# SyncE issue times that depend on pair sums in a build-time planner, and new order rules for its last quarter

## Chip, cores and metric

The kernel runs on one core of a Trainium2 chip. The metric is the time of one execution in device microseconds (us); the number compared is the median of several runs. One further execution is taken with the hardware profiler, and its trace is what the profile below is made of.

## The reference, cut to what is computed

```python
xn = layernorm(x)                       # x: 1 x 2048 x 640
q = (xn @ wq)  -> 32 heads of 20;  k = xn @ wk;  v = xn @ wv     # one K and V for all heads
p = softmax(q k^T * 20**-0.5)           # 32 x 2048 x 2048
attn = (p v, heads side by side) @ wo
h = relu(xn @ w1 + b1) ** 2             # 640 -> 1536
return x + attn + (h @ w2 + b2)
```

All inputs and the output are bf16.

## The kernel before, in words

**Tiles.** The attention is cut into 32 *blocks*, one for each of 4 query chunks (512 queries) times 8 groups of 4 heads. A block has 16 key tiles x 4 heads = 64 score tiles of 128 x 512, so 2048 in all. TensorE makes a score tile in one of the 8 PSUM banks; two paths turn it into exponentials:

- **ScalarE path**: steps `QK0` to `QK695` make 2 tiles each, and one ACTIVATE (L1020) takes the exponential of both. 1392 tiles go this way. `PV<block>_<key tile>` are the matmuls that multiply them with V.
- **Set path**: 164 *sets* of 4 tiles (one key tile, 4 heads). `DQK<set>_<head>` makes the scores, `D1_<set>_<i>` on VectorE (L1232) writes a scaled integer whose bits are a rough bf16 exponential, and three *passes* `P1` to `P3` add constants to those bits, on GpSimd (`int64_add`, L1252) or on VectorE (L1254). The four terms are multiplied with V or with a scaled V and added up in PSUM (`DPV<block>_<key tile>_<term>`). A **pair sum** `AD0` or `AD3` adds two of the terms before that, which saves one `DPV`: as a DMA that accumulates 512 KB from SBUF into SBUF, issued by GpSimd (L1267), or on VectorE (L1272).

**End of a block.** `TN` (VectorE, L1101) copies the block's result out of PSUM. Then a chain through memory divides by the sums of the softmax: SyncE issues `SM` (L1103, sums to DRAM) and 4 or 5 `OM` (L1124, the heads' rows to their places); `SL` (L1105) reads the sums back, spread over 128 partitions; `RC` (VectorE reciprocal, L1107) inverts them; `RS` (L1108) writes them out; `BC` (L1130) broadcasts them; `CM` (VectorE, L1137) multiplies. SyncE is one in-order queue of DMA issues, which also has `QD` (L733, queries to their places), `FR` (L766), `OD` (L814, output rows) and `XD30` (L1094). Blocks 30 and 31 are divided on VectorE without memory (L1082 to L1099).

**Other work.** Between attention matmuls TensorE fills in the projections (`QC`), the first MLP matmul (`FFN`, evacuated by `RL`, squared by `SQ`), and `OUT16` to `OUT23`, each of 17 chunks of 4 matmuls (MLP second matmul and `wo`), evacuated by `OE` (L838). The last four row tiles end in the tail: `OF<row>_<half>_<chunk>` (5 chunks of 4 matmuls for each of 8 halves), `PA` (L1327) and `OFe` (L1332, L1334).

**What sets the order.** Nothing is ordered by hand around the change. When the kernel is built, a planner (the `while True` loop, and `commit`, L194) plays the engines forward with a planned duration for each operation, picks the next operation by planned start and priority, and appends it to its engine's list. The chip then runs each list strictly in order, with semaphore waits where data comes from another engine or a DMA. Planned durations do not reach the chip; they only decide the order. On SyncE they are constants: 0.62 for `SM`, 0.6 for `SL`, `RS` and `BC`, 0.95 for `OM`, 0.9 for `QD`, 0.45 for `OD`, 0.7 for `FR`. `dma_free` is the planned time until which the DMA engines are taken by pair sums (2.73 us each, `ADGAP`) and other transfers.

`RULES` holds, for each 10 us *stage* of the planned ScalarE time, the planner's parameters that differ from `DEFAULTS`: priorities (`PVA`, `PVD`, `SQP`), how many sets may be open (`NOPEN`), how many pair sums per set go by DMA (`ADDM`) or to VectorE (`ADDN`), how readily passes go to VectorE (`PBIAS`), and others.

Of the kernel before, what the change touches and what calls it, by code (L numbers as in the profile page):

```python
# [28 lines left out]
EPS = 1e-5  # L29
# [9 lines left out]
def _pl(z):  # L39
# [61 lines left out]
KEEP = 3  # L101
# [50 lines left out]
         53: {'DRATE': 0.8, 'ND': 1, 'ADPM': 2.4},
         54: {'DRATE': 0.8, 'EPS': 0.03, 'R3': 9, 'PVA': 1, 'ND': 1, 'ADPM': 2.4},
         55: {'DRATE': 0.8, 'PP': 0.9, 'QKP': -0.5},
         56: {'DRATE': 0.8, 'M1T': 0, 'ADDN': 0, 'ADDB': 1, 'SQP': 0.7, 'ADDM': 0},
         57: {'DRATE': 0.8, 'M1T': 0, 'ADDN': 0, 'ADDB': 1, 'SQP': 0.7, 'ADDM': 0},
         58: {'PVA': 0.9},
         59: {'DRATE': 0.95, 'IDLE': 0.15, 'URG': 4, 'EPS': 0.03, 'ADP': 2, 'D1P': 0.3, 'PP': 4, 'SQP': 0.7, 'ND': 1, 'KEEP': 0, 'ADPM': 2.4, 'KEEPX': 2, 'DVL': 2.4},
         60: {'DLAST': 2, 'EPS': 0.06, 'DQP': 1.5, 'ADDM': 1},
         61: {'EVP': 0.8, 'DGAP': 0, 'DRATE': 0.95, 'IDLE': 0.15, 'URG': 4, 'ADP': 5, 'PVA': 0.9, 'PP': 4, 'KEEP': 0, 'ADPM': 2.4, 'DVL': 2.4},  # L160
         62: {'EVP': 0.3, 'DGAP': 1.5, 'DRATE': 0.95, 'BEHIND': 0.12, 'IDLE': 0.15, 'NOPEN': 3, 'EPS': 0.06, 'MRG': 1, 'M1': 0, 'ADP': 3.5, 'JIT': 0.7, 'PVA': 0.9, 'D1P': 0.3, 'PP': 4, 'SQP': 2, 'DQP': 0.5, 'KEEP': 2, 'ADDM': 1.5, 'ADPM': 2.4, 'KEEPX': -1, 'DVL': 0.9, 'P2': 2},
         63: {'EVP': 0.3, 'DGAP': 1.5, 'DRATE': 0.95, 'BEHIND': 0.12, 'IDLE': 0.15, 'NOPEN': 3, 'EPS': 0.06, 'MRG': 0, 'M1': 0, 'ADP': 5, 'JIT': 0.7, 'PVA': 0.9, 'D1P': 0.3, 'PP': 4, 'SQP': 2, 'DQP': 0.5, 'KEEP': 1, 'ADDM': 1.5, 'ADPM': 2.4, 'KEEPX': -1, 'DVL': 0.9, 'P2': 2},
# [11 lines left out]
MPRIO = 0.9  # L174
BEHIND = 0.3
IDLE = 0.3
# [21 lines left out]
                M1T=2, ADDN=0, ADDB=0, ADP=0.9, JIT=0.9, R3=9, PVA=1, PVD=1.05, D1P=1, PP=2.5, SQP=0.7, DQP=3, QKP=0, ND=3, WARM=0.72,  # L198
                KEEP=1, ADDM=0.8, ADPM=0.9, KEEPM=0, KEEPX=4, DVL=1.2, P2=0)
# [66 lines left out]
def bass_parallel_sum__grouped_kv_mqa__dense_activation_squared_relu__prompt_kernel(nc, A_x, A_wq, A_wk, A_wv, A_wo, B_x, B_w1, B_b1, B_w2, B_b2, out):  # L266
    es = ExitStack()
    with es:
# [1099 lines left out]
        while True:  # L1368
# [313 lines left out]
```

## Time and profile before

| what | value |
|---|---|
| median of 3 runs (lowest to highest) | 669.46 us (669.13 to 669.87) |
| the profiled execution's own time | 670.66 us |
| its span, first to last instruction | 668.8 us |
| mean granted TensorE clock | 0.997 |
| pair sums by DMA | 67 + 56 + 5 of 512 KB, and 2 more from x_sb to tmore |

The profile's span is 1.9 us shorter than the execution it belongs to, and that execution is 1.2 us longer than the median. Busy shares are averages over the span; what ends a stretch is read from the idle time in front of an instruction, and the name behind the arrow there is what released it. "SPq" rows are SyncE's DMA issues: their duration is the issue, not the transfer.

### The profile page before, as it was taken

How to read it: one execution, taken by the hardware profiler on the slowest of the kernel's cores; microseconds unless marked ns; L12 is line 12 of the kernel's file. 1: busy time of each engine (PE TensorE's matmuls, PEld its weight loads, DVE VectorE, ACT ScalarE, POOL GpSimd, SP SyncE). 2: the span in 40 equal slices, each digit the busy share in tenths (PEclk: the TensorE clock that was granted, in tenths of full speed). 3: DMA queues.
4: the chain of work that ended last, by engine and by line, in shares of the span. 5: the costliest groups of instructions: out<-in, count | busy, mean ns of one | idle time of the engine just before them, and what ended most of it. 6: DMA issues, size and time to landing. Idle time of an engine off the chain costs nothing.

```text
span 668.8 us, 22416 instructions
## 1 busy us (share of the span) xinstructions
PE 661.0 (99%) x9602; PEld 210.7 (32%) x9603; DVE 602.8 (90%) x1081; ACT 651.4 (97%) x719; POOL 578.5 (87%) x592
## 2 busy tenths in 40 slices
PE   8999999999999999999999999999999999999898
PEld 4532222333322223333332222333332222223245
DVE  8979999999999999999989999988999999998654
ACT  6999999999999999999999999999999999999895
POOL 1619999999999999999899999999998998999761
PEclk9999999999999999999999999999999999999999
DMA  8897755787877987777788676668786976177875
GB/s 253 257 248 173 161 125 98 161 176 159 178 157 140 192 164 154 158 150 164 143 173 166 121 139 137 134 143 162 146 168 134 180 146 122 24 147 161 173 155 124
DMA packets 54360, 104.71 MB, mean 157 GB/s; under 512 B 16108, under 2 KB 31356, under 8 KB 54196
## 3 DMA queue, kind: packets, MB, share of 16 engines
q0 software_dynamic: 19376, 70.79, 56.8%
q1 hardware_dynamic: 34308, 32.11, 16.9%
q8 instruction: 75, 1.23, 0.8%
q10 hardware_dynamic: 576, 0.38, 0.2%
q14 instruction: 25, 0.20, 0.1%
HBM read 23.26 MB, written 10.01 MB: 50 GB/s over the span
## 4 chain that ended last, share of the span: by engine, by line
PE 88%; POOL 4%; DVE 3%; DMA 3%; SPq 1%; issue 1%; DVEq 0%; POOLq 0%
PE ps L429 86%; POOL x_sb L1252 2%; POOL tmore L1252 2%; DMA x_sb<-tmore 1%; PE ps L604 1%; DMA tmore<-tmore 1%; DVE tmore L1232 1%; PE ps L633 1%; SPq L1130 1%; DMA R<-drs 1%; SPq L1124 1%; DVE hT_tmp L753 0%; POOL tmore L1267 0%; POOL x_sb L1267 0%; PE ps L663 0%
## 5 line engine op out<-in xcount | busy, mean ns | idle before, releaser
L1020 ACT ACTIVATE PT<-ps 128x1024 bf16<-128x1024 f32 x696 | 642.2, 1066 | 5.1 <-PE ps L429 4.7
L1232 DVE TENSOR_SCALAR tmore<-ps 128x512 uint16<-128x512 f32 x656 | 424.5, 683 | 36.1 <-PE ps L429 28.1
L1252 POOL INT64_ADD tmore<-tmore x220 | 241.7, 1199 | 31.4 <-DVE QCr L707 10.2
L429 PE MATMUL ps<-qT,kT 20*128 20x512 bf16 x2048 | 265.2, 385 | 0.1
L1252 POOL INT64_ADD x_sb<-tmore x217 | 240.5, 1224 | 17.2 <-PE ps L429 7.2
L429 PEld LDWEIGHTS ps<-qT,kT 20*128 20x128 bf16 x2048 | 66.3, 91 | 254.1 <-ACT PT L1020 220.6
L429 PE MATMUL ps<-PT,vx 128*32 128x512 bf16 x1392 | 133.0, 388 | 0.0
L429 PE MATMUL ps<-w_sb,big 128*32 128x320 bf16 x1536 | 77.4, 305 | 2.0 <-DVE tmore L1232 2.0
L429 PE MATMUL ps<-xnT,w_sb 128*32 128x512 bf16 x960 | 77.3, 383 | 0.3 <-DVE tmore L1232 0.2
L1267 POOL DMA_DIRECT2D tmore<-tmore x67 | 68.4, 1036 | 3.3 <-POOL tmore L1252 2.1
L1267 POOL DMA_DIRECT2D x_sb<-tmore x56 | 62.0, 1123 | 2.1 <-POOL x_sb L1252 2.1
L429 PE MATMUL ps<-tmore,vxs 128*32 128x512 bf16 x632 | 57.3, 382 | 0.0
L429 PE MATMUL ps<-x_sb,vxs 128*32 128x512 bf16 x624 | 56.0, 382 | 0.3 <-POOL x_sb L1252 0.3
L429 PEld LDWEIGHTS ps<-PT,vx 128*32 128x32 bf16 x1392 | 33.4, 93 | 63.8 <-issue 58.0
L429 PE MATMUL ps<-tmore,vx 128*32 128x512 bf16 x512 | 48.7, 382 | 0.0
L429 PEld LDWEIGHTS ps<-w_sb,big 128*32 128x32 bf16 x1536 | 33.9, 96 | 30.7 <-issue 18.4
L753 DVE TENSOR_SCALAR hT_tmp<-ps,b1col 128x512 bf16<-128x512 f32 x48 | 35.6, 741 | 1.1 <-PE ps L429 1.0
L429 PE MATMUL ps<-xnT,wq_sb 128*32 128x512 bf16 (+2 forms) x480 | 33.3, 356 | 0.0
L429 PE MATMUL ps<-x_sb,vx 128*32 128x512 bf16 x328 | 32.1, 382 | 0.0
L429 PE MATMUL ps<-wo_c,OC 128*32 128x320 bf16 x576 | 29.8, 301 | 0.0
L429 PEld LDWEIGHTS ps<-xnT,w_sb 128*32 128x32 bf16 x960 | 18.3, 94 | 26.8 <-issue 20.6
L1254 DVE TENSOR_SCALAR x_sb<-tmore 128x2048 uint16<-128x2048 uint16 x28 | 22.0, 790 | 0.0
(97 smaller groups left out, 318.9 us busy)
## 6 DMA issues: line engine op xcount, KB each, us to landing
tmore<-tmore POOLq DMA_DIRECT2D x67, 512.0 KB, 5.5
x_sb<-tmore POOLq DMA_DIRECT2D x56, 512.0 KB, 5.6
w_sb<-in_B_w_dram SPq DMA_DIRECT2D x8, 480.0 KB, 11.5
big<-OR SPq DMA_DIRECT2D x71, 40.0 KB
xb<-in_A_x_dram SPq DMA_DIRECT2D x1, 2560.0 KB, 12.6
xb<-b2r POOLq DMA_DIRECT2D x1, 2560.0 KB, 19.9
xr<-xb SPq DMA_DIRECT2D x16, 160.0 KB, 4.3
x_sb<-x_sb POOLq DMA_DIRECT2D x5, 512.0 KB, 4.8
```

Source lines behind the costliest of these rows:

```text
L429: return lambda e: e.matmul(out_, l, r, start=start, stop=stop, tile_position=tp, skip_group_check=loose)
L604: return [lambda e: e.matmul(ps[:, PVB, :], ones_bf[:, :], hT_tmp[:, 0, :], start=True, stop=True)]
L633: return [(lambda e, dt=dt: e.transpose(out=psbf(bk)[:, dt * 128:(dt + 1) * 128], in_=xn_sb[:, st, dt:D:DT], identity=ident[:])) for dt in ...
L753: o = Op(f"RL{qc}_{f}", "DVE", 0.66, [lambda e: e.tensor_scalar(out=hT_tmp[:, k % 2, :], in0=ps[:, bk, :], scalar1=b1col[:, f:f + 1], scal ...
L1020: return Op(f"ACT{st_['j']}", "ACT", ACB + ACM * n, [lambda e: e.activation(out=PT[:, s0:s0 + n, :], in_=ps[:, b0:b0 + (n - 1) * db + 1:db ...
L1124: dd = wide(op(f"OM{b}_{j}", "SP", 0.95, lambda e, p0=p0, n=n, sl=sl, j=j, o0=o0: e.dma_start(cbuf(2 * sl)[p0:p0 + n, :], OR[32 * j + o0:3 ...
L1130: bc = wide(op(f"BC{b}_{j0}", "SP", 0.6, lambda e, p0=p0, n=n, m=m, sl=sl, j0=j0: e.dma_start(cbuf(2 * sl + 1)[p0:p0 + n, :], drs[b, 1][51 ...
L1232: d1 = op(f"D1_{n}_{i}", "DVE", 0.60, lambda e: e.tensor_scalar(out=L[:, cs].bitcast(U16), in0=ps[:, bank, :], scalar1=XA, scalar2=XB, op0 ...
L1252: fn = lambda e, T=T, j=j: e.int64_add(out=T.bitcast(I64), in0=L.bitcast(I64), in1=TSTEP * j * 0x0001000100010001)
L1254: fn = lambda e, T=T, j=j: e.tensor_scalar(out=T.bitcast(U16), in0=L.bitcast(U16), scalar1=TSTEP * j, scalar2=None, op0=ALU.add)
L1267: p = op(f"AD{a}_{n}", "POOL", ADDUR, lambda e, src=src, dst=dst: e.dma_start(dst, src, accum_op=ALU.add), dp + [ad_last.get(k)], dma=adse ...
```

## The change

Two things change in the planner; no operation's code changes.

1. **SyncE durations.** In `commit`, each SyncE operation with a planned start after 560 us gets its planned duration multiplied: by 1.3 if `dma_free` lies 1.0 to 2.9 us, or at least 4.0 us, ahead of the start, and by 0.84 otherwise.
2. **Rules.** The entries of `RULES` for stages 50 to 66 (planned ScalarE time from 490 us on) are replaced; stage 52 now has none.

```diff
+SPF, SPG, SPT = 1.3, 0.84, 560.0
 DWQ, DWO, DWB, DWS, DWM, DWOD, DOFF = 0.02, 0.22, 0.16, 0.02, 0.16, 1.0, 1.28
...
-         50: {'DGAP': 0.3, 'M1T': 0, 'PVD': 1.2, 'DVL': 0.9},
...
-         65: {'MPRIO': 0.9, 'BEHIND': 0.3, 'IDLE': 0.6, 'MRG': 0, 'KEEPX': 1},
-         66: {'MPRIO': 0.9, 'BEHIND': 0.3, 'IDLE': 0.6, 'MRG': 0, 'KEEPX': 1}}
+         50: {'EVP': 0.3, 'DGAP': 1.5, 'DRATE': 0.95, 'BEHIND': 0.12, 'IDLE': 0.15, 'NOPEN': 3, ...
+         51: {'EVP': 0.8, 'PBIAS': 3, 'DRATE': 0.95, 'NOPEN': 3, 'M1T': 1.2, 'ADP': 3.5, 'JIT': 0.8, ...
...
+         62: {'ADDN': 0.5},
...
+         65: {'EVP': 0.8, 'DGAP': 0.8, 'DLAST': 6, 'DRATE': 0.95, 'BEHIND': 0.12, 'IDLE': 0.3, 'URG': 2, ...
+         66: {'ADDB': 1, 'P2': 1}}
...
             if op.eng == "PE":
                 pe_mode[0] = op.mode
                 pe_log.append((s, s + op.dur))
+            if op.eng == "SP" and s > SPT:
+                op.dur *= SPF if 1.0 <= dma_free[0] - s < 2.9 or dma_free[0] - s >= 4.0 else SPG
             op.start, op.fin = s, s + op.dur
```

In the two built programs the lists are the same up to `QK523` on TensorE, the end of block 23 on VectorE, set 125 on GpSimd and `OM23_2` on SyncE. Behind that every list is in another order. ScalarE's list is the same throughout. The number of steps (696), of sets (164), of operations on SyncE (501) is the same.

More of the change, by code (lines that the diff above doesn't have):

```diff
@@ L148 @@
          49: {'EVP': 0.3, 'DGAP': 0.8, 'DLAST': 6, 'DRATE': 0.95, 'BEHIND': 0.12, 'IDLE': 0.3, 'URG': 2, 'EPS': 0.06, 'MRG': 1, 'M1T': 1.2, 'JIT': 0.8, 'PVA': 0.9, 'ND': 2, 'KEEP': 0, 'KEEPM': 2, 'KEEPX': -1, 'DVL': 99},
-         50: {'DGAP': 0.3, 'M1T': 0, 'PVD': 1.2, 'DVL': 0.9},
-         51: {'EVP': 0.8, 'DRATE': 0.95, 'URG': 4, 'M1T': 1.2, 'ADP': 3.5, 'JIT': 0.7, 'PVA': 0.9, 'D1P': 0.5, 'SQP': 3, 'ND': 2, 'KEEPM': 2, 'KEEPX': 1},
-         52: {'EVP': 0.8, 'DRATE': 0.95, 'NOPEN': 3, 'M1T': 1.2, 'ADP': 3.5, 'JIT': 0.8, 'PVA': 0.9, 'SQP': 3, 'ND': 2, 'KEEPX': 4},
@@ L152 @@
[L152 to L162, printed above, removed]
@@ L163 @@
-         64: {'EVP': 0.3, 'DGAP': 0.8, 'DLAST': 6, 'DRATE': 0.95, 'BEHIND': 0.12, 'IDLE': 0.3, 'EPS': 0.06, 'MRG': 1, 'M1T': 1.2, 'ADDN': 0.2, 'JIT': 0.8, 'PVA': 0.9, 'D1P': 0.5, 'DQP': 0.5, 'ND': 2, 'KEEP': 0, 'KEEPM': 2, 'KEEPX': -1, 'DVL': 99},
-         65: {'MPRIO': 0.9, 'BEHIND': 0.3, 'IDLE': 0.6, 'MRG': 0, 'KEEPX': 1},
-         66: {'MPRIO': 0.9, 'BEHIND': 0.3, 'IDLE': 0.6, 'MRG': 0, 'KEEPX': 1}}
+         50: {'EVP': 0.3, 'DGAP': 1.5, 'DRATE': 0.95, 'BEHIND': 0.12, 'IDLE': 0.15, 'NOPEN': 3, 'EPS': 0.06, 'MRG': 1, 'M1': 0, 'ADP': 3.5, 'JIT': 0.7, 'PVA': 0.9, 'D1P': 0.3, 'PP': 4, 'SQP': 2, 'DQP': 0.5, 'KEEP': 2, 'ADDM': 0.6, 'ADPM': 2.4, 'KEEPM': 1, 'KEEPX': -1, 'DVL': 0.9, 'P2': 2},
@@ new lines @@
+         51: {'EVP': 0.8, 'PBIAS': 3, 'DRATE': 0.95, 'NOPEN': 3, 'M1T': 1.2, 'ADP': 3.5, 'JIT': 0.8, 'PVA': 0.9, 'SQP': 3, 'ND': 2, 'KEEPX': 4},
+         53: {'EPS': 0.12, 'MRG': 1, 'R3': 2},
+         54: {'EPS': 0.12, 'MRG': 1, 'R3': 2, 'ND': 1},
+         55: {'DRATE': 0.8, 'NOPEN': 4, 'EPS': 0.03, 'R3': 9, 'PVA': 1, 'ND': 1, 'ADPM': 2.4},
+         56: {'DRATE': 0.8, 'NOPEN': 4, 'EPS': 0.03, 'R3': 9, 'PVA': 1, 'D1P': 3, 'ND': 1, 'ADPM': 2.4},
+         57: {'PBIAS': 8, 'BEHIND': 0.3, 'EPS': 0.12, 'MRG': 1, 'ADP': 2, 'KEEP': 0},
@@ new lines @@
+         58: {'BEHIND': 0.3, 'PP': 0.9, 'DQP': 0.5},
+         59: {'EPS': 0.12, 'MRG': 1, 'KEEP': 0, 'DVL': 1.8},
+         60: {'EVP': 0.8, 'DRATE': 0.95, 'URG': 4, 'M1T': 1.2, 'ADP': 3.5, 'JIT': 0.7, 'PVA': 0.9, 'D1P': 0.5, 'SQP': 3, 'ND': 2, 'KEEPM': 2, 'KEEPX': 1},
+         61: {'PVA': 1, 'PVD': 1.5, 'QKP': -0.5, 'KEEP': 3},
+         62: {'ADDN': 0.5},
+         63: {'EVP': 0.3, 'MPRIO': 0.3, 'DGAP': 0.8, 'DLAST': 6, 'DRATE': 0.95, 'BEHIND': 0.12, 'IDLE': 0.3, 'NOPEN': 4, 'EPS': 0.06, 'MRG': 0, 'M1T': 1.2, 'JIT': 0.8, 'PVA': 0.9, 'QKP': 0, 'ND': 2, 'KEEPM': 2, 'KEEPX': -1, 'DVL': 99},
@@ L166 @@
+         64: {'EVP': 0.3, 'MPRIO': 0.3, 'DGAP': 0.8, 'DLAST': 6, 'DRATE': 0.95, 'BEHIND': 0.12, 'IDLE': 0.3, 'NOPEN': 4, 'EPS': 0.06, 'MRG': 0, 'M1T': 1.2, 'PVA': 0.9, 'QKP': 0, 'ND': 2, 'KEEPM': 2, 'KEEPX': -1, 'DVL': 99},
+         65: {'EVP': 0.8, 'DGAP': 0.8, 'DLAST': 6, 'DRATE': 0.95, 'BEHIND': 0.12, 'IDLE': 0.3, 'URG': 2, 'MRG': 0, 'M1T': 1.2, 'ADDB': 1, 'JIT': 0.8, 'PVA': 0.9, 'ND': 2, 'KEEP': 0, 'KEEPM': 2, 'KEEPX': -1, 'DVL': 0.9, 'P2': 0},
+         66: {'ADDB': 1, 'P2': 1}}
 HOOK = None
```

## The prediction

> **What bounds the kernel now.** I read the busy shares first, then stages, then the stages in which the busiest engines fall off.
>
> ```profile
> PE 661.0 (99%) x9602; PEld 210.7 (32%) x9603; DVE 602.8 (90%) x1081; ACT 651.4 (97%) x719; POOL 578.5 (87%) x592
> ```
> ```profile
> 400.00:500.00 100.00, 99.94 (x1467) 30.86 (x1459) 91.23 (x154) 100.00 (x110) 95.10 (x96) 1.00 0.73 147
> ...
> 600.00:620.00 20.00, 20.00 (x317) 6.86 (x317) 18.12 (x32) 20.00 (x22) 18.62 (x19) 1.00 0.81 166
> 620.00:640.00 20.00, 18.04 (x283) 6.59 (x275) 10.84 (x20) 16.74 (x19) 14.50 (x15) 0.91 0.75 157
> 640.00:660.00 20.00, 20.00 (x402) 9.63 (x402) 10.23 (x18) 19.57 (x22) 9.73 (x10) 1.00 0.78 165
> ```
>
> The columns are stage and length, then busy time (and instructions) of PE, PEld, DVE, ACT, POOL, then granted clock, DMA share, GB/s. TensorE and ScalarE are both full nearly everywhere. ScalarE's 696 steps are the same in both kernels, so where it is full no order can gain. The one stage in which it isn't is 620 to 640 us. Its own timeline says how much it loses there, and how little elsewhere in the re-ordered part:
>
> ```profile
> 569.74 11.46 ACT L1020 ACTIVATE PT<-ps 128x1024 bf16<-128x1024 f32 x12 [0.20 <-PE ps L429]
> 581.41 51.62 ACT L1020 ACTIVATE PT<-ps 128x1024 bf16<-128x1024 f32 x56 [0.21 <-PE ps L429]
> 635.42 1.94 ACT L1020 ACTIVATE PT<-ps 128x1024 bf16<-128x1024 f32 x2 [2.38 <-PE ps L429]
> 638.24 21.34 ACT L1020 ACTIVATE PT<-ps 128x1024 bf16<-128x1024 f32 x23 [0.88 <-PE ps L429]
> ```
>
> It loses 2.38 + 0.88 = **3.26 us** at one place and 0.20 + 0.21 = 0.41 us in the rest. What TensorE waited for, and what that waited for, is in the timeline of that place:
>
> ```profile
> 619.53 0.56 SPq L1103 DMA_DIRECT2D drs<-OR  x1
> 620.13 0.45 SPq L814 DMA_DIRECT2D out_dram<-out_sb  x1
> 620.62 2.53 SPq L1124 DMA_DIRECT2D big<-OR  x2
> 623.20 2.64 SPq L1130 DMA_DIRECT2D cmore<-drs  x2
> 625.88 1.59 SPq L1130 DMA_DIRECT2D big<-drs  x1
> 627.51 1.57 SPq L1124 DMA_DIRECT2D big<-OR  x2
> 629.13 0.48 SPq L1105 DMA_DIRECT2D R<-drs  x1
> ```
> ```profile
> 633.26 0.25 DVE L1107 RECIPROCAL R<-R 128x16 f32<-128x16 f32 x1 [3.09 <-DMA R<-drs]
> ...
> 634.12 0.72 PE L429 MATMUL ps<-w_sb,big 128*32 128x320 bf16 x8 [1.96 <-DVE tmore L1232]
> ```
>
> This is `RC29`. SyncE needs from 619.53 to 629.13 = 9.60 us to get from `SM29` to `SL29`, with the three `BC28` in between; `SL29` lands at 633.26; VectorE, in order, sits for 3.09 us; the `D1` behind it doesn't empty its bank; TensorE stops for 1.96 us, and ScalarE runs dry. By the planner's constants those nine issues take 0.62 + 0.45 + 4 x 0.95 + 3 x 0.6 = 6.67 us: the queue was 2.9 us later than planned, which is the wait.
>
> The rest of ScalarE's loss is clock:
>
> ```profile
> 632.00:634.00 2.00, 0.16 (x4) 0.00 (x0) 0.73 (x3) 1.04 (x2) 1.69 (x2) 1.00 0.08 27
> 634.00:635.00 1.00, 0.88 (x12) 0.25 (x12) 1.00 (x3) 0.00 (x0) 0.00 (x0) 0.57 0.95 184
> 635.00:636.00 1.00, 1.00 (x16) 0.31 (x16) 0.26 (x1) 0.58 (x1) 0.63 (x1) 0.50 1.11 199
> ...
> 637.00:638.00 1.00, 1.00 (x21) 0.41 (x12) 0.00 (x0) 0.36 (x1) 1.00 (x3) 0.73 0.09 18
> ```
>
> After the pause TensorE runs some 3.4 us at half clock. So a pause of 1.96 us on TensorE cost 3.26 us on ScalarE, 1.66 us for each. The Trainium skill, "TensorE: Matmul & The Clock Gate", section "What's actually happening", gives about 3.4 us of idle as the window after which the clock halves; by it a pause of 1.96 us would cost itself alone, and new pauses of that size would be priced at 1.0 instead of 1.66 for each us. The rows differ: the clock fell after 1.96 us.
>
> **The change part by part.** *Longer issues while a pair sum moves.* The constants reach the chip only as an order, so first: are they nearer the truth? SyncE's `QD` rows of two windows, and of the DMA queues in the first of them the row of q0, the queue of the pair sums:
>
> ```profile
> 529.31 8.31 SPq L733 DMA_DIRECT2D qT<-QCr  x7
> ...
> 574.98 4.50 SPq L733 DMA_DIRECT2D qT<-QCr  x6
> ```
> ```profile
> q0 software_dynamic: 256, 0.91, 57.5%
> ```
>
> The row is that of 529.3 to 537.6; from 574.9 to 581 the view has no q0 row. One `QD` takes 8.31 / 7 = 1.19 us beside sums and 4.50 / 6 = 0.75 us without. The new plan takes 0.9 x 1.3 = 1.17 and 0.9 x 0.84 = 0.76. That is right within 2%. The Trainium skill, "Perfetto Trace Analysis", section "DMA Instruction — HWDGE (DVE, Sync)", speaks against it: the profiled issue is lock wait, descriptor generation and semaphore push, and the data's movement lies outside. By it a moving sum need not lengthen an issue; that is the third rival below.
>
> *The stall.* In the new order the three `BC28` and `OM29` change places: `SM29`, four `OM29`, `FR1`, `RS28`, `OD8`, `SL29`, then `BC28`. `SL29` now waits for `RS28`, so for `RC28`, which moved on VectorE from ahead of `TN29` to nine places behind it; from `RC28` to `RC29` stand nine operations (seven `D1`, a pass, `CM3_1`).
>
> ```profile
> 641.29 1.25 DVE L1232 TENSOR_SCALAR tmore<-ps 128x512 uint16<-128x512 f32 x2
> ```
> ```profile
> 640.06 1.15 SPq L814 DMA_DIRECT2D out_dram<-out_sb  x1
> ```
>
> Two `D1` in a row take 1.25 us, so nine such operations some 9 x 0.62 = 5.6 us. In it go `RS28` 0.33 to 1.65, `OD8` 0.45 to 1.15, and `SL29` until it has landed:
>
> ```profile
> L1105 SPq DMA_DIRECT2D R<-drs x8: 429/1024/1394, 489.2 to 629.1; - x8
> ...
> L1108 SPq DMA_DIRECT2D drs<-R x8: 319/520/1650, 504.3 to 633.5; - x8
> ...
> DMA to landing us min/median/max: 1.4/4.0/7.1
> ```
>
> From `RC28` that is 0.33 + 0.45 + 4.0 = 4.8 us at best pace and 1.65 + 1.15 + 7.1 = 9.9 at worst (`OD` at its longest, before the tail, is the 1.15 above). So `RC29` waits between 0 and 4.3 us. What is queued behind it differs: before, `D1_161_3`, whose bank TensorE needs; now `OE18`, `AD3_160`, `OE19`, `TN30`. All four tiles of set 161 and one of 162 are ahead of it, the next `D1` is due after step 678, and `RC29` after step 662. The last chunk of `OUT18`, which `OE18` waits for, stands behind step 669. Step to step is 0.93 us (21.34 / 23), so 7 steps or 6.5 us lie between. Even the worst case is covered: I take **-3.26 us** (between -3.26 and 0).
>
> *The tail.* After the last `PV31_11` TensorE had one more `DPV` and 39 `OF` chunks; now it has no `DPV` and 35. VectorE has one `PA` fewer behind the last transposes.
>
> ```profile
> 662.71 1.26 DVE L1327 TENSOR_TENSOR ps<-ps,w_sb 128x320 f32<-128x320 f32 x3
> ...
> 666.05 0.49 DVE L1334 TENSOR_TENSOR PT<-ps,w_sb 128x320 bf16<-128x320 f32 x1 [0.32 <-PE ps L429]
> ```
> ```profile
> 661.23 0.58 PE L429 MATMUL ps<-wo_c,OC 128*32 128x320 bf16 x12
> 661.64 0.31 PE L429 MATMUL ps<-w_sb,OC 128*32 128x320 bf16 x4
> ```
>
> Three chunks take 661.64 - 661.23 = 0.41 us, so four are 0.55 us of TensorE; one `PA` is 0.40 us of VectorE. The end waits for both by turns (0.32 us on PE). I take 0.5 for it and 0.2 for the `DPV` (four matmuls of 512 columns, where a chunk has four of 320: 0.137 x 512 / 320 = 0.22): **-0.7 us** (between 0 and -1.2).
>
> *Work that is added.* GpSimd issues one more pair sum in all, VectorE makes one more, TensorE has two `DPV` fewer. By sets it shifts more: sets 135 to 154 get 16 sums by DMA instead of 12, and 55 passes on GpSimd instead of 57; sets 155 to 163 get 8 instead of 10.
>
> ```profile
> 530.00:605.00 75.00, 74.62 (x957) 20.26 (x949) 71.52 (x123) 74.52 (x81) 68.85 (x71) 1.00 0.57 114
> ```
> ```profile
> L1252 POOL INT64_ADD tmore<-tmore x30 | 31.9, 1164 | 3.0 <-PE ps L429 1.0 <-DVE tmore L1254 1.0 <-DVE big L761 1.0
> ...
> L1267 POOL DMA_DIRECT2D tmore<-tmore x7 | 6.6, 941 | 1.3 <-PE ps L429 1.3
> L1267 POOL DMA_DIRECT2D x_sb<-tmore x6 | 6.5, 1086 | 0.6 <-POOL x_sb L1252 0.6
> ```
>
> In the 75 us that hold sets 135 to 154 GpSimd is busy 68.85. It gains 4 x 1.0 and loses 2 x 1.2: 70.5, with 4.5 us of idle as cover. VectorE gains two passes, 1.3 us, on 71.52. I cost it at nothing; if the cover is gone it is the slower rival. The extra sum on VectorE lies where it is half idle (10.23 of 20), and takes 1.23 us:
>
> ```profile
> 654.48 1.23 DVE L1272 TENSOR_TENSOR tmore<-tmore 128x2048 bf16<-128x2048 bf16 x1 [2.37 <-POOL tmore L1252]
> ```
>
> *Another order from 495 us on.* Every wait that an order can make is unknown until it runs. From below: none, and the 0.41 us there now go too. From above: one wait like `RC29`'s, 3.26 us. I counted steps between a set's last score tile and the first use of each term, in both built orders from set 126 on: for pair sums by DMA the least is 12 before and 12 after; for plain passes 4 and 5. So nothing gets tighter, and I take the value near the small waits of the same stretch: **+0.5 us**.
>
> Sum: -3.26 - 0.7 + 0.5 = **-3.5 us**: span 668.8 to 665.3, the profiled execution 670.66 to 667.2, and, that execution being 1.2 us over the median, the median 669.46 to **666.0 us**.
>
> **The rivals.**
> - *The wait moves.* Some other in-order wait (an `RC`, a `CM`, or a `DPV` on a late sum) takes 1.5 to 3.3 us of ScalarE. For: the profile shows that one late landing does it, and `RC29` is still behind a chain of 4.8 to 9.9 us. Against: the counts above. Time 666.0 + 1.0 to 2.8 = 667.0 to 668.8.
> - *Slower: GpSimd becomes the bound* between 530 and 605 us, because the four extra sums run long.
>
> ```profile
> 615.54 1.85 POOL L1267 DMA_DIRECT2D x_sb<-tmore  x1
> ```
>
>   At 1.85 us each they add 4 x 1.85 - 2.4 = 5.0 to 68.85: 73.9 of 75. It decides from 75 on: then all later passes come late, `DPV`s wait for them in order, and TensorE's pauses cost 1.66 for each us. A shortfall of 3 us is 5.0 of ScalarE: 666.0 + 5.0 = 671.0. Against: 4.5 us of cover at the mean durations.
> - *It doesn't do what it says.* If issues are not long because of sums, the order is merely another one with a late `SL29` and a wait of its own: 669.5 less the tail at most, 668.8 to 669.5. Against: 1.19 and 0.75.
>
> **How the numbers follow.** Forecast 0.55, the wait moves 0.22, GpSimd 0.18, not what it says 0.05. A measurement of this kernel can tell about 0.2%, 1.34 us, from no change: faster is below 668.1, slower above 670.8. Faster are the forecast and 0.14 of the moved wait: 0.69. Slower is 0.15 of the GpSimd case. Within are the other 0.08 and 0.03 of these two and the 0.05: 0.16. The range begins where all goes right (-3.26 - 1.2 - 0.41 is 664.6, less likely than 664.8) and goes up through the moved wait and the third rival to 670.5, which leaves out most of the GpSimd case.
>
> **What would show it.** ScalarE's timeline from 495 us on in pieces without the 2.38 and 0.88; granted clock 1.00 between 620 and 640 us; `RC29` with a wait below 4.3 us and no idle of TensorE behind it; last reciprocal to end shorter by 0.5. I am wrong if ScalarE shows over 2 us of idle at another place, or GpSimd over 74 of 75 us between 530 and 605.

## The result and the profile after

| | before | changed |
|---|---|---|
| median (lowest to highest) | 669.84 us (669.13 to 670.78), 7 runs | 667.10 us (666.44 to 670.22, and one at 2331.58), 7 runs |
| the profiled execution | 670.66 us | 666.88 us |
| its span | 668.8 us | 665.1 us |
| mean granted clock in it | 0.997 | 1.000 |

The ratio is 0.9961, with a 95% interval of 0.9943 to 0.998: faster by 0.4%. The execution of 2331.58 us had a granted clock of 0.236; it was disturbed, and the ratio leaves it out (the median of the other six is 666.99). The forecast was 666.0 us in a range of 664.8 to 670.5.

Lines of the changed kernel stand two further down than in the kernel before (L429 is now L431, L1107 is L1109). First its busy shares, from the head of its page:

```profile
PE 657.5 (99%) x9598; PEld 210.0 (32%) x9599; DVE 606.8 (91%) x1082; ACT 650.6 (98%) x719; POOL 579.0 (87%) x593
```

The shares tell little: ScalarE's work fell by 0.8 us while the span fell by 3.7. The stages show where it went. Columns as before: stage and length, then busy time of PE, PEld, DVE, ACT and POOL, granted clock, DMA share, GB/s.

```profile
530.00:605.00 75.00, 73.48 (x956) 19.81 (x952) 72.58 (x123) 74.12 (x81) 70.50 (x73) 1.00 0.74 144
600.00:620.00 20.00, 19.82 (x313) 6.76 (x309) 19.07 (x33) 20.00 (x23) 18.65 (x20) 1.00 0.78 157
620.00:640.00 20.00, 20.00 (x386) 8.74 (x378) 14.44 (x25) 20.00 (x23) 15.66 (x16) 1.00 0.89 187
640.00:660.00 20.00, 19.88 (x427) 10.09 (x423) 10.75 (x19) 16.65 (x20) 7.91 (x8) 1.00 0.40 93
```

Between 620 and 640 us ScalarE is now full (20.00, was 16.74) and the clock is 1.00 (was 0.91). Its last steps now end before 660, so the 16.65 in the last row is the tail coming earlier. But 530 to 605 has a new loss: ScalarE is at 74.12 of 75, where it was at 74.52, and TensorE at 73.48, where it was at 74.62. ScalarE's timeline gives each idle time with its place:

```profile
496.25 71.88 ACT L1022 ACTIVATE PT<-ps 128x1024 bf16<-128x1024 f32 x78 [0.71 <-PE ps L431]
568.96 87.58 ACT L1022 ACTIVATE PT<-ps 128x1024 bf16<-128x1024 f32 x95 [0.82 <-PE ps L431]
```

Idle of 0.20 + 0.21 + 2.38 + 0.88 = 3.67 us has become 0.71 + 0.82 = 1.53. The last 95 steps run without a stop, 0.922 us each. At that pace the 81 steps that took from 581.41 to 659.58 before would have taken 74.7 us instead of 78.17: the stall at `RC29` cost 3.5 us in that execution.

The sum of the span: 2.14 us of listed idle gone; 0.74 of idle too short to be listed, inside the groups of steps (steps and gaps from 439 us on took 220.21 - 3.67 = 216.54 before and 217.33 - 1.53 = 215.80 now, for the same 234 steps); 0.16 from the start of the kernel; and the tail. From the last exponential's end to the end of the span it was 668.8 - 659.58 = 9.22 us and is 665.1 - 656.54 = 8.56: 0.66 less. Together 3.7.

SyncE's issues around block 29, in its own timeline, show the reordering at work:

```profile
616.74 0.56 SPq L1105 DMA_DIRECT2D drs<-OR  x1
617.34 4.56 SPq L1126 DMA_DIRECT2D big<-OR  x4
621.94 1.30 SPq L768 DMA_DIRECT2D w_sb<-fpd  x1
623.28 0.49 SPq L1110 DMA_DIRECT2D drs<-R  x1
623.81 0.43 SPq L816 DMA_DIRECT2D out_dram<-out_sb  x1
624.29 0.43 SPq L1107 DMA_DIRECT2D R<-drs  x1
628.59 1.43 SPq L1132 DMA_DIRECT2D cmore<-drs  x2
```

From `SM29` to `SL29` are 624.29 - 616.74 = 7.55 us instead of 9.60, and the `BC28` come behind. On VectorE's timeline `RC29` still waits, and so does `OE18` behind it:

```profile
629.08 0.26 DVE L1109 RECIPROCAL R<-R 128x16 f32<-128x16 f32 x1 [1.66 <-DMA R<-drs]
631.36 0.49 DVE L840 TENSOR_TENSOR out_sb<-ps,xr 128x320 bf16<-128x320 f32 x1 [2.02 <-PE ps L431]
```

`RC29` waits 1.66 us for its landing; then `OE18` waits 2.02 us more for matmuls. Nobody needed VectorE in that time, and neither TensorE nor ScalarE stops here. The two new idle times of ScalarE come from elsewhere. At 494 us, in the timeline of all engines:

```profile
494.24 1.89 DVE L1234 TENSOR_SCALAR tmore<-ps 128x512 uint16<-128x512 f32 x3 [1.09 <-DMA tmore<-tmore]
...
494.99 0.39 PE L431 MATMUL ps<-qT,kT 20*128 20x512 bf16 x1 [0.52 <-DVE tmore L1234]
```

VectorE sat 1.09 us for a pair sum to land. This place is still in the part of the lists that both kernels share, so the change didn't bring it. And at 568 us, in the re-ordered part:

```profile
565.96 0.88 POOL L1269 DMA_DIRECT2D x_sb<-tmore  x1 [1.26 <-DVE tmore L1234]
566.56 2.37 POOL L1254 INT64_ADD x_sb<-tmore  x2
...
567.98 0.40 PE L431 MATMUL ps<-x_sb,vxs 128*32 128x512 bf16 x4 [1.09 <-POOL x_sb L1254]
```

A `DPV` stands 1.09 us on TensorE for its pass `P3_142`, which is late on GpSimd, behind a gap of 1.26 us ahead of a sum's issue.

### The profile page after: what moved, and what is told of

Its sections match the earlier page's. It is cut to its first block, busy times and chain, and to the rows that moved or that the text cites. A ratio compares the mean times of both kernels' runs of the same rounds, so it can differ in the third digit from the quotient of the medians.

```text
span 665.1 us, 22426 instructions
## 1 busy us (share of the span) xinstructions
PE 657.5 (99%) x9598; PEld 210.0 (32%) x9599; DVE 606.8 (91%) x1082; ACT 650.6 (98%) x719; POOL 579.0 (87%) x593
## 4 chain that ended last, share of the span: by engine, by line
PE 90%; POOL 6%; DVE 2%; DMA 1%; issue 1%; DVEq 0%; POOLq 0%
PE ps L431 87%; POOL tmore L1254 3%; POOL x_sb L1254 2%; DMA tmore<-tmore 1%; DVE tmore L1234 1%; PE ps L606 1%; PE ps L635 1%; POOL tmore L1269 0%; PE ps L665 0%; PE ps L563 0%; DVE OC L1139 0%; PE ps L568 0%; POOL x_sb L1269 0%; PE ps L592 0%; DVE QCr L1101 0%
## 5 line engine op out<-in xcount | busy, mean ns | idle before, releaser
L431 PE MATMUL ps<-qT,kT 20*128 20x512 bf16 x2048 | 263.8, 384 | 0.9 <-DVE tmore L1234 0.5
L431 PEld LDWEIGHTS ps<-qT,kT 20*128 20x128 bf16 x2048 | 65.9, 91 | 255.3 <-ACT PT L1022 226.5
L431 PE MATMUL ps<-PT,vx 128*32 128x512 bf16 x1392 | 132.3, 387 | 0.0
L431 PE MATMUL ps<-xnT,w_sb 128*32 128x512 bf16 x960 | 77.1, 383 | 0.2 <-DVE tmore L1234 0.2
L431 PE MATMUL ps<-w_sb,big 128*32 128x320 bf16 x1536 | 75.3, 301 | 0.1
L431 PE MATMUL ps<-tmore,vxs 128*32 128x512 bf16 x636 | 57.7, 382 | 0.0
L431 PE MATMUL ps<-x_sb,vxs 128*32 128x512 bf16 x624 | 56.2, 382 | 1.3 <-POOL x_sb L1254 1.3
L431 PEld LDWEIGHTS ps<-PT,vx 128*32 128x32 bf16 x1392 | 33.5, 93 | 61.9 <-issue 55.0
L431 PE MATMUL ps<-tmore,vx 128*32 128x512 bf16 x500 | 47.4, 382 | 0.0
L431 PEld LDWEIGHTS ps<-w_sb,big 128*32 128x32 bf16 x1536 | 33.2, 95 | 28.3 <-issue 18.8
L431 PE MATMUL ps<-xnT,wq_sb 128*32 128x512 bf16 (+2 forms) x480 | 33.1, 356 | 0.0
L431 PE MATMUL ps<-x_sb,vx 128*32 128x512 bf16 x328 | 32.2, 382 | 0.0
L431 PE MATMUL ps<-wo_c,OC 128*32 128x320 bf16 x576 | 29.7, 301 | 0.0
L431 PEld LDWEIGHTS ps<-xnT,w_sb 128*32 128x32 bf16 x960 | 18.5, 94 | 27.1 <-issue 20.6
L840 DVE TENSOR_TENSOR out_sb<-ps,xr 128x320 bf16<-128x320 f32 x24 | 11.7, 487 | 12.3 <-PE ps L431 12.3
```

What stands on the lines that cost most here:

```text
L431: return lambda e: e.matmul(out_, l, r, start=start, stop=stop, tile_position=tp, skip_group_check=loose)
L840: o = Op(f"OE{n}", "DVE", 0.40, [lambda e: e.tensor_tensor(out=out_sb[:, slot, cs], in0=ps[:, bk, 0:HW], in1=xrow(st, cs), op=ALU.add)], [ ...
```

## The experiments

**The theory (A):** the gain is `SL29`'s place in SyncE's queue, so `RC29`'s landing, plus the shorter tail. **Its main rival (B):** the gain comes from the rest of the new order (other sums, other passes, fewer `DPV`), and `RC29` is only where the lateness used to show. In the expectations A and B are these two, or the two answers that the run's question leaves. Runs were made in three groups, each beside runs of the kernel before, whose medians were 669.91 us (e0 to e3, 14 runs), 670.29 (e4 to e7, 23) and 670.68 (e8 to e10, 27). Ratios are to the group's own.

All edits that move operations act on the finished order, just ahead of where it is dealt out to the engines, and change nothing else:

```python
moved = [o for o in order_all if o.name in NAMES]
order_all[:] = [o for o in order_all if o.name not in NAMES]
at = next(k for k, o in enumerate(order_all) if o.name == AHEAD_OF)
order_all[at:at] = moved
```

### e0: the changed kernel again

No edit; it is the yardstick for e1 to e3.

> The changed kernel once more, for the spread of its own runs. Theory A (the gain is the wait at the reciprocal of block 29 that is gone, plus a shorter tail) and theory B (the new rules give an altogether better order) both expect a ratio of 0.993 to 0.998 to the kernel before. What it tells apart is something else: two of six earlier runs of this kernel took 668.7 and 670.2 us at a granted clock of 0.997, the others 666.4 to 667.1 at 1.000. If a wait appears in some executions only, this run shows both values again.

666.52 us (665.89 to 668.49, 6 runs), ratio 0.995 (0.9935 to 0.9965). Its profile has a span of 664.6 us and, in ScalarE's timeline, one listed idle time from 480 us to the tail:

```profile
568.50 87.55 ACT L1022 ACTIVATE PT<-ps 128x1024 bf16<-128x1024 f32 x95 [0.77 <-PE ps L431]
```

The wait at 568 us is a property of the order (it is 0.83, 0.78 and 0.78 in e2, e4 and e6); the one at 496 is not there, so it belongs to single executions (e5's profile has 0.62 us there). One of the six runs, at 668.49 us, has a mean clock of 0.997; the other five have 1.000 and a median of 666.51.

### e1: SyncE's factors with the old rules

```diff
+SPF, SPG, SPT = 1.3, 0.84, 560.0
+            if op.eng == "SP" and s > SPT:
+                op.dur *= SPF if 1.0 <= dma_free[0] - s < 2.9 or dma_free[0] - s >= 4.0 else SPG
```

> Only the first half of the change: SyncE's planned durations with the new factors, RULES as before. Its order has 165 sets and 694 ScalarE steps. Theory A: SL29 now stands ahead of the three BC28, but RC29 comes only some 17 VectorE operations (10 us) after TN29 and the D1 behind it is urgent, so a wait of 0 to 3 us stays; the rules were not chosen for this order, so small waits come on top: ratio 0.996 to 1.004. Theory B (rules do it): no gain, 1.000 to 1.006. If it comes out at 0.9955 or less, the factors alone are the change.

672.90 us (672.19 to 673.86, 6 runs), ratio 1.0042 (1.0029 to 1.0055): slower, just above what theory A expected and within B's 1.000 to 1.006. The planner now makes 165 sets and 694 steps. ScalarE's timeline, then TensorE's from the last steps on:

```profile
570.96 84.06 ACT L1023 ACTIVATE PT<-ps 128x1024 bf16<-128x1024 f32 x91 [0.20 <-PE ps L432]
667.01 1.42 ACT L1335 ACTIVATE out_sb<-ps 128x320 bf16<-128x320 f32 x4 [11.99 <-PE ps L432]
```
```profile
654.36 1.80 PE L432 MATMUL ps<-w_sb,big 128*32 128x320 bf16 x48
655.99 0.85 PE L432 MATMUL ps<-wo_c,OC 128*32 128x320 bf16 x20
...
657.10 1.80 PE L432 MATMUL ps<-w_sb,big 128*32 128x320 bf16 x48
658.73 0.85 PE L432 MATMUL ps<-wo_c,OC 128*32 128x320 bf16 x20
```

The stall is gone here too: the last exponential ends at 570.96 + 84.06 = 655.02, with two steps fewer even earlier than in the changed kernel. But two whole row tiles (48 + 20 matmuls each, 655.99 + 0.85 - 654.36 = 2.5 us, so 5.0) are still to be done on TensorE from 654.36 on, and ScalarE then idles 11.99 us; the tail is 671.5 - 655.02 = 16.5 us. What the planner had saved at the stall it lost by leaving filler work to the end. The factors alone make the kernel slower.

### e2: the new rules without the factors

```diff
-SPF, SPG, SPT = 1.3, 0.84, 560.0
+SPF, SPG, SPT = 1.0, 1.0, 560.0
```

> Only the second half: the new RULES, with factors of 1.0. The built order differs from that of the changed kernel in one exchange on SyncE (RS26 and OM27_1) and one on TensorE (QK620 and DPV28_13_1). Both theories: the same time as the changed kernel within 0.1%, ratio to before 0.993 to 0.998. If it is above 0.9985, that one exchange matters, which neither theory has.

666.93 us (666.07 to 667.9, 6 runs), ratio 0.9955 (0.9941 to 0.9969): the changed kernel's time. The built lists differ from the changed kernel's by two swaps: `RS26` with its neighbour `OM27_1` on SyncE, and on TensorE the two `DPV` on either side of `QK620`, `DPV28_12_2` and `DPV28_13_1`. So with these rules the longer issue times decide nothing on the chip. The first half of the change is inert in the final order; if it did anything, it was in the search for the rules.

### e3: before, with SL29 ahead of the BC28

```diff
+NAMES, AHEAD_OF = ("SL29",), "BC28_0"     # in the kernel before
```

> The kernel before, with one operation moved in the finished lists: SL29 stands ahead of the three BC28 and the last two OM29, everything else as it was. Theory A: SL29 is issued about 6 us earlier, RC29 doesn't wait, ScalarE's 2.38 + 0.88 us of idle and the half clock behind it go: 3.0 to 3.9 us less, 665.6 to 666.6 us, ratio 0.994 to 0.9955; the tail stays at 9.2 us from the last exponential to the end. Theory B: less than 1 us, ratio above 0.9985.

668.40 us (668.0 to 669.8, 8 runs), ratio 0.998 (0.9969 to 0.9992): only part of it, and not the 665.6 to 666.6 of theory A. In its profile (span 666.5) the stall at `RC29` is gone, as the first row shows, which has no wait; the other rows, of the same timeline, show another one 14 us later and the issue of the sum behind it:

```profile
630.21 0.24 DVE L1107 RECIPROCAL R<-R 128x16 f32<-128x16 f32 x1
...
636.25 1.81 POOL L1267 DMA_DIRECT2D tmore<-tmore  x2
...
644.40 0.40 PE L429 MATMUL ps<-tmore,vxs 128*32 128x512 bf16 x4 [1.12 <-DMA tmore<-tmore]
...
645.16 1.02 ACT L1020 ACTIVATE PT<-ps 128x1024 bf16<-128x1024 f32 x1 [1.01 <-PE ps L429]
```

A `DPV` of block 31 waits for the pair sum `AD3_160`, issued at 636.25 and landed at 644.36, 8.1 us later. Before, the stall at 633 us had hidden it. The last exponential ends at 657.30 instead of 659.58: the move took out 3.3 us and gave back 1.0. Theory A was too simple by one wait.

### e4: the changed kernel, with the BC28 back ahead of SL29

```diff
+NAMES, AHEAD_OF = ("BC28_0", "BC28_3"), "SL29"     # three DMAs, in the changed kernel
```

> The changed kernel, with the three BC28 moved ahead of SL29 again, everything else as it was. In the changed kernel's profile BC28_0 sat until 628.6 us for the landing of RS28, so SL29 goes out at about 630.6 instead of 624.3 and RC29 waits some 8 us instead of 1.7; behind RC29 there were 2.0 us of idle before OE18. Theory A (the chain of block 29 is what the gain hangs on, and the new order has some 4 us of room at RC29): the room is used up, OE18, TN30 and then CM3_3 come 2 to 4 us later, and 2 to 4 us of the gain go: 668.5 to 671 us. Theory B (the rules as a whole): within 0.5 us of the changed kernel, 666.5 to 667.5.

668.54 us (667.17 to 674.26, 12 runs), ratio 0.9983 (0.9963 to 1.0003): most of the gain is gone. Its timeline:

```profile
631.91 0.25 DVE L1109 RECIPROCAL R<-R 128x16 f32<-128x16 f32 x1 [5.07 <-DMA R<-drs]
632.08 0.43 DVE L840 TENSOR_TENSOR out_sb<-ps,xr 128x320 bf16<-128x320 f32 x1
...
632.57 0.39 PE L431 MATMUL ps<-qT,kT 20*128 20x512 bf16 x2 [0.86 <-DVE out_sb L840]
```

`SL29` is issued at 628.55, `RC29` waits 5.07 us, `OE18` behind it is now late, and a `QK` stands 0.86 us for its bank; ScalarE loses 0.85. The profile's span is 665.7, only 0.6 longer than the changed kernel's, where 2 to 4 us had been expected to go. But in 5 of the 12 runs the mean granted clock is 0.995 to 0.997, and these take 668.93 to 674.26 us, where the other seven take 667.17 to 668.61, with a median of 667.65.

So the order of these four DMAs matters, but the twelve runs' median overstates it. At a clock of 1.000 the runs of before in this group have a median of 669.50, and e4 still gains 1.85 us on them with the `BC28` ahead of `SL29`. The new order has a second way to keep `RC29` from stopping TensorE: in the changed kernel's profile what stands behind `RC29` could be 1.66 + 2.02 = 3.7 us late at no cost, and only what went beyond that was lost here. This run speaks for A, and for a part of B.

### e5: the changed kernel, with SL29 earlier still

```diff
+NAMES, AHEAD_OF = ("SL29",), "FR1"     # in the changed kernel
```

> The changed kernel, with SL29 moved ahead of FR1, RS28 and OD8: it is issued at about 622 instead of 624.3 us, and the 1.66 us that RC29 still waits go. Theory A says that wait is covered (VectorE has nothing due behind it for 2 us more, no idle of TensorE or ScalarE follows): the time stays within 0.3 us of the changed kernel, 666.3 to 667.2. The rival, that what is left of the wait still costs, expects 1.0 to 1.7 us less, 665 to 666.

667.32 us (666.58 to 668.25, 6 runs), ratio 0.9954 (0.9938 to 0.9969): no difference that can be told (0.1 us above the range of theory A, and far from its rival's 665 to 666). VectorE's timeline:

```profile
628.68 0.24 DVE L1109 RECIPROCAL R<-R 128x16 f32<-128x16 f32 x1
632.70 0.49 DVE L840 TENSOR_TENSOR out_sb<-ps,xr 128x320 bf16<-128x320 f32 x1 [3.78 <-PE ps L431]
```

`RC29` waits no more, and `OE18` waits 3.78 us instead of 2.02 for its matmuls: the 1.66 us were covered. The cover was about 3.8 us in all, and with e4's 5.07 it is exceeded.

This profile also shows, by chance, what half clock costs. The wait at 568 us is there with the same size on TensorE, 1.08 us; but here the clock fell behind it. TensorE's row at the pause, ScalarE's timeline and the stages of this run, and below them the same stage of the changed kernel:

```profile
567.87 0.55 PE L431 MATMUL ps<-x_sb,vxs 128*32 128x512 bf16 x4 [1.08 <-POOL x_sb L1254]
```
```profile
569.42 1.02 ACT L1022 ACTIVATE PT<-ps 128x1024 bf16<-128x1024 f32 x1 [1.35 <-PE ps L431]
571.36 86.52 ACT L1022 ACTIVATE PT<-ps 128x1024 bf16<-128x1024 f32 x94 [0.92 <-PE ps L431]
```
```profile
568.00:570.00 2.00, 2.00 (x19) 0.40 (x15) 0.68 (x2) 0.65 (x2) 2.00 (x3) 0.50 1.01 196
570.00:572.00 2.00, 2.00 (x22) 0.34 (x14) 1.35 (x3) 1.08 (x2) 2.00 (x3) 0.65 0.55 119
```
```profile
568.00:570.00 2.00, 2.00 (x30) 0.59 (x34) 1.25 (x3) 1.16 (x2) 2.00 (x3) 1.00 1.03 202
```

With the clock at 0.50 TensorE did 19 matmuls in those 2 us instead of 30, and ScalarE idled 1.35 + 0.92 = 2.27 us instead of 0.82. Half clock behind the pause cost 1.45 us, more than the pause.

### e6: the changed kernel, with the last PV ahead of four OF chunks

```diff
+NAMES, AHEAD_OF = ("PV31_11",), "OF12_0_1"     # in the changed kernel
```

> The changed kernel, with PV31_11 moved four OF chunks earlier on TensorE, as it nearly stood before. Theory A (the tail is bound by TensorE's chunks behind the last PV): TensorE waits for the last exponential with four chunks still to do, and the end comes 0.3 to 0.55 us later; from the last exponential to the end of the span 8.9 to 9.1 us instead of 8.56. Rival (the tail is bound by VectorE's chain alone, or its gain came from elsewhere): no change, 8.5 to 8.6 us. The difference is under what the medians can tell; the profile decides.

667.19 us (666.6 to 670.76, 12 runs), ratio 0.9962 (0.9948 to 0.9975). In medians that can't be told from the changed kernel. ScalarE's timeline:

```profile
568.28 87.82 ACT L1022 ACTIVATE PT<-ps 128x1024 bf16<-128x1024 f32 x95 [0.78 <-PE ps L431]
```

The last exponential ends at 656.10 and the span at 665.3: the tail is 9.2 us again instead of 8.6. The four chunks were worth 0.6 us at this place.

### e7: e3, with the late sum's DPV moved back

```diff
+NAMES, AHEAD_OF = ("DPV31_15_2",), "PV31_5"     # added to e3
```

> The kernel before with SL29 moved ahead of BC28 (the earlier run that came to 668.4 us and showed a new wait of 1.01 us on ScalarE at 645 us, where TensorE sat for a pair sum that took 8.1 us to land), and DPV31_15_2, the matmuls that waited for that sum, moved two ScalarE steps later. Theory A' (the gain of the one move was eaten by the next late landing): the 1.01 us go, 667.2 to 667.8 us, and ScalarE's timeline from 582 us on is one piece. Rival (the wait turns up at the next place again, as the order has no room in it): 668.0 to 668.6 with idle of about 1 us at another step.

667.26 us (666.56 to 668.14, 6 runs), ratio 0.9952 (0.9935 to 0.9969): the changed kernel's time, from the kernel before with one DMA and one group of four matmuls moved. All six runs have a granted clock of 1.000. ScalarE's timeline is now without a listed idle time behind 572 us:

```profile
572.40 84.22 ACT L1020 ACTIVATE PT<-ps 128x1024 bf16<-128x1024 f32 x91 [0.18 <-PE ps L429]
```

The tail is still 665.8 - 656.62 = 9.2 us. This is the strongest evidence for A: the two late landings on the path make up the gain but for the tail, as far as medians of six runs can tell (e5 and e6 have 667.32 and 667.19 in the same group), and the rest of the new order is not needed for it. It is not the only way to that gain: e4 shows that the new order brings cover of its own.

### e8: e5, with the DPV at 568 us moved back

```diff
+NAMES, AHEAD_OF = ("DPV27_12_3",), "FFN2_5.2"     # added to e5
```

> The changed kernel with SL29 early (which by itself changed nothing) and DPV27_12_3 moved two ScalarE steps later. In four of five profiles of this order ScalarE showed 0.77 to 0.83 us of idle at 568 us, where TensorE sat 1.1 us for the last pass of set 142 on GpSimd, which that matmul reads. Theory A (each single late landing costs what ScalarE shows): 0.8 us less than the changed kernel, 665.7 to 666.4, no idle of ScalarE at 568. Rival (the wait moves to the matmul behind it, DPV27_13_1 or DPV27_11_1): 666.4 to 667.3 with 0.5 to 0.8 us of idle within ten steps.

666.81 us (665.82 to 668.32, 10 runs), ratio 0.9938 (0.9919 to 0.9957). The median is above the 665.7 to 666.4 of theory A and within its rival's 666.4 to 667.3. ScalarE's timeline in its profile, of the fastest run (span 663.9):

```profile
570.68 1.02 ACT L1022 ACTIVATE PT<-ps 128x1024 bf16<-128x1024 f32 x1 [0.17 <-PE ps L431]
572.03 1.94 ACT L1022 ACTIVATE PT<-ps 128x1024 bf16<-128x1024 f32 x2 [0.33 <-PE ps L431]
574.25 81.11 ACT L1022 ACTIVATE PT<-ps 128x1024 bf16<-128x1024 f32 x88 [0.28 <-PE ps L431]
```

The 0.8 us at 568 is gone, and 0.17 + 0.33 + 0.28 = 0.78 us stands 2 to 6 us later: the wait moved, as the rival had it. The ratio is the lowest of all, but its interval overlaps the changed kernel's, and the runs of before beside it lost the clock most often (19 of 27), which lowers the ratio; in microseconds e0 had 666.52. A better version, perhaps, and not shown to be one.

### e9: e7, with four OF chunks ahead of the last PV

```diff
+NAMES, AHEAD_OF = ("OF12_0_1", "OF12_0_2", "OF12_0_3", "OF12_1_0"), "PV31_11"     # added to e7
```

> The kernel before with the two moves that brought it to 667.3 us (SL29 early, DPV31_15_2 late), and the tail's part of the change: four OF chunks moved ahead of PV31_11. Theory A: from the last exponential to the end 8.7 to 8.9 us instead of 9.2 (one DPV still follows the last PV), 666.5 to 667.0 us; three moves of one to four operations are then all of the change's gain. Rival (the new rules hold something more): it stays at 667.2 or above.

668.02 us (667.4 to 670.25, 12 runs), ratio 0.9959 (0.9942 to 0.9976): a miss, by 1 us. The last exponential ends at 656.12, the span at 665.9: the tail is 9.8 us, longer. VectorE's timeline shows the transposes of the last block waiting longer for TensorE (0.51 us in e7):

```profile
657.59 0.72 DVE L1082 STREAM_TRANSPOSE OR<-ps 128x512 f32<-128x512 f32 x1 [1.05 <-PE ps L429]
```

In the order of before TensorE is still busy with earlier work when the last exponentials end, so whatever is put ahead of the last `PV` delays the final chain: ScalarE ended 0.50 us earlier than in e7, and the last `PV` still started at 656.93, where it was 656.89. In the changed kernel the same chunks ahead of it gain 0.6 us; with them behind it (e6), TensorE waits 0.27 us for the last exponential before that `PV`. So the tail's gain is not the four chunks as such: it needs a TensorE that has less left to do at that point.

### e10: before, with the pause filled

```diff
+at = next(k for k, o in enumerate(order_all) if o.name == "OUT19.0")
+order_all[at:at] = [Op("fill", "PE", 0.224, fill_parts()) for k in range(8)]
```

`fill_parts` gives four matmuls with zeros as weights, which add nothing to their bank.

> The kernel before, with eight groups of matmuls by zero (1.8 us) put on TensorE ahead of OUT19, where it paused 1.96 us in the profile. The wait for RC29 stays. Of 23 runs of the kernel before in one call, 11 had a mean clock of 0.997 and took 670.2 to 671.8 us, 12 one of 1.000 and 668.6 to 671.4. Theory C (in half of the executions the pause also halves the clock, which costs about 1.4 us more): no run at 0.997, all between 668.6 and 669.8, median 0.4 to 1 us under that of the kernel before; ScalarE idle about 2 to 2.5 us in all at 633. Rival (the clock falls elsewhere, or costs nothing): clocks of 0.997 in some runs as before, same spread.

669.31 us (668.71 to 672.23, 12 runs), ratio 0.9991 (0.9971 to 1.001). The fill ran (its row is the first), TensorE's pause shrank from 1.96 to 0.83 us, and the stage behind it, in the second fence, has a granted clock of 1.00 where it was 0.57:

```profile
631.31 1.90 PE L429 MATMUL ps<-kT,zeros 128*32 128x512 bf16 x32
633.19 0.25 DVE L1107 RECIPROCAL R<-R 128x16 f32<-128x16 f32 x1 [3.69 <-DMA R<-drs]
...
634.04 0.46 PE L429 MATMUL ps<-w_sb,big 128*32 128x320 bf16 x8 [0.83 <-DVE tmore L1232]
```
```profile
634.00:635.00 1.00, 0.96 (x20) 0.36 (x24) 1.00 (x2) 0.14 (x1) 0.00 (x0) 1.00 1.08 205
```

`RC29` waited even longer than before, 3.69 us, yet ScalarE lost 2.50 us and not 3.26. In 1 of the 12 runs the mean granted clock was below 0.999; of the kernel before's 27 runs in the same group it was in 19. So the fill mostly keeps the clock and leaves the wait; the ratio alone can't show the gain, since its interval includes 1. Two things were not as theory C had them: four runs are above its 669.8, one of them at 0.997, and the ten runs at 1.000 have a median of 669.3, where the seven runs of before that kept it have 668.80, so the fill shows no gain in executions that keep the clock anyway.

## Why the prediction was right, and where it was off

**The stall: right in place and cause, too large for the median.** The step was "I take **-3.26 us** (between -3.26 and 0)". `RC29`'s stall went (e3 and e7 show that in the order of before `SL29`'s place makes it), and in the profiled executions it was worth 3.5 us. But the profiled execution of before was one with half clock. Over e0 to e3 and e4 to e7 the runs of before with a mean clock of 1.000 have medians of 669.45 and 669.50 us (9 and 12 runs), those with 0.997 or less 671.08 and 671.06 (5 and 11): about 1.6 us is half clock, and only some of the executions have it. (In the group of e8 to e10 it is 668.80 and 671.10, 7 and 19 runs: 2.3.) The median run of before lost some 3.26 - 1.6 = 1.7 us at that place when the clock held, or 1.0 by the third group. The prediction's "1.66 for each" us of pause is a price of some executions, not of all. The change also makes the loss of the clock rarer: it is at 0.997 in 3 of the changed kernel's 12 undisturbed runs, here and in e0, and at 0.997 or less in 35 of 64 of before.

**Its cover: right that it held, wrong by how much.** `RC29`'s wait was 1.66 us, within the 0 to 4.3 given, and it was covered (e5). The cover was put at 6.5 us, counted in steps; the changed kernel shows 3.7 and e5 3.8, and with 5.07 us of wait (e4) time was lost. The worst case of the prediction, 4.3 us, would not have been free.

**One landing is not the end of it.** The prediction looked for what comes next in the new order and not in the old one. e3 shows that in the order of before the sum behind the stall was late by another 1.1 us; the new order happened to have removed that too (e7).

**The tail: right.** -0.7 forecast, -0.66 in the spans, and e6 puts 0.6 of it on the four chunks' place. The prediction priced the chunks as work on TensorE that vanishes; e9 shows that this holds only where TensorE has time to spare ahead of the last step.

**New waits: mis-sized.** +0.5 forecast, net of the old 0.41: 1.53 - 0.41 = 1.12 us in the profile; of the 1.53, 0.82 belongs to the new order and 0.71 to that execution. The counts of steps were the wrong measure for it. They said that plain passes have no less time than before (5 steps, was 4), but the pass that was late at 568 us was late behind a gap on GpSimd that no count shows.

**GpSimd: right.** 70.5 us forecast for 530 to 605, 70.50 in the profile, with 4.5 us of it idle as forecast. The 0.82 us on ScalarE come from one late pass, not from a full engine.

**"It doesn't do what it says": half right, at a chance of 0.05.** The issue times are nearer the truth in the two rows that the prediction shows, less clearly in the changed kernel's profile: there `QD` rows take 0.80 us each (from 534.57) and 0.95 (from 570.18) while the queue of the pair sums has 43.6% and 72.0% of the DMA engines, where the prediction's row beside sums took 1.19. And e2 shows that they decide nothing in the final order, and e1 that with the old rules they make the kernel slower. Only the outcome that was tied to this (668.8 to 669.5) was wrong, because the order that came with it is a good one.

**The sum.** The span was forecast at 665.3 and is 665.1; the median at 666.0, and it is 667.10 beside 669.84 of before, or 666.52 beside 669.91 (e0). In ratios: 0.9948 forecast (666.0 over 669.46), 0.9961 (0.9943 to 0.998) and 0.995 (0.9935 to 0.9965) measured. That the span agrees to 0.2 us is in part luck: -3.26 + 1.12 - 0.66 is -2.8, and the other 0.9 is the 0.74 of short idle and the 0.16 of the start, for which the prediction had no term. So is the median: the full 3.26 of a half-clock execution was taken off a median that lost less at that place, and in the runs at a clock of 1.000 e0 gains 669.45 - 666.51 = 2.9 us. The difference from a profile to a median is the clock: the profile of before happened to be an execution that had lost it, the profile after one that had kept it.

**Open.** The 1.26 us gap on GpSimd at 565 us isn't explained: the row names a `D1` of VectorE as its releaser, but the kernel before has a gap of 1.25 us at 563.5, ahead of the same sum of the set before (`AD0_141`), whose row names TensorE. No experiment took either away. Nor is it settled whether e8 is faster than the changed kernel.

## What to carry to other kernels

When a stall is long, ask whether the clock fell behind it in that execution, and price it twice: a single profile shows either the one or the other, and a median is a mixture. In an in-order DMA queue, put the short transfer that someone waits for ahead of those that nobody waits for yet, or see to it that what stands behind the waiter can be late (e4); then look at once for the next late landing in the old order, which the stall had hidden. Before a planner's better constants are credited, build the order with and without them: here they exchanged two pairs of operations.

## What the runs showed of the hardware

- **The clock can fall behind a pause of 1.1 us, and need not.** The same `DPV` stood 1.09 us in the changed kernel's profile and 1.08 in e5's; the granted clock of the next 2 us was 1.00 in the one and 0.50 in the other. By e5's two rows, at 0.50 and 0.65, the half clock lasted 2 + 2 x 0.35 / 0.5 = 3.4 us. Behind 1.96 us it fell in the profile of before, and in 35 of the 64 runs of before in the three groups the mean clock was 0.997 or less. The Trainium skill, "TensorE: Matmul & The Clock Gate", section "What's actually happening", calls the window in which activity is watched free-running, so that the same kernel varies with where it falls. That agrees with the two profiles. Its figure of about 3.4 us of idle ahead of half clock doesn't: 1.08 us were enough here.
- **Pair sums can land late.** A sum of 512 KB was under way for 8.1 us in e3, where the median of the kernel before is 5.5; one that VectorE waits for at 494 us was late in one execution of the changed kernel and not in another (0.71 us of ScalarE, or nothing).
- **Runs of one kernel spread by more than its edits do.** The changed kernel's six runs go from 666.44 to 670.22 us, while e5, e6, e7 and e2 lie within 0.4 us of one another in their medians. Below about 0.2% only the rows of a profile tell edits apart.
